# Large attention scores of batches 2 to 7 over 64 rows, two heads side by side in the array

## The chip, the cores and the metric

The kernel runs on one core of a Trainium2 chip. A core has a matrix engine (TensorE, "PE" in the profile, with its weight loads listed apart as "PEld"), VectorE (DVE), ScalarE (ACT), GpSimd (POOL) and SyncE (SP), which issues most transfers. The engines have queues of their own and wait for each other by semaphores. The metric is the device time of one execution in microseconds (us): the median over several executions. A change of under 0.2% is about what can't be told from none.

## The reference

Attention with 8 batches, 8 heads, 576 positions and a head dimension of 64, then a mixer over tokens and channels:

```
scores = q @ k^T / sqrt(64)
mask: 0 <= rel < 32                        for heads 0 to 3  (plain)
      0 <= rel < 128 and rel % 4 == 0      for heads 4 to 7  (dilated)
x = softmax(scores under the mask) @ v     -> (batch, 576, 512)
u = x + (relu(x^T @ w_tok1) @ w_tok2)^T
out = u + relu(u @ w_ch1) @ w_ch2
```

Here rel is the query position less the key position. Input and output are float32; the kernel computes in float16 with sums in float32.

## The kernel before

**Score blocks.** Only blocks near the diagonal are computed, with the keys on the 128 partitions of the output and the queries along the row. For a plain head there are three large blocks of 128 keys x 160 queries, and small blocks for the end. For a dilated head positions are taken by their remainder modulo 4, and the large blocks are four of 128 x 128. The tiles of the large blocks are `sc`, one PSUM bank for each head; the small blocks of both heads of a pair share one bank, `sm`.

**Pairs of heads.** Two heads lie on top of each other: `kt[hp]` holds the transposed keys of pair `hp`, head 0 in rows 0 to 63 and head 1 in rows 64 to 127. `qz[hp]` has the transposed queries twice, at index `h` of its second axis: for head 0 rows 64 to 127 are zero, for head 1 rows 0 to 63. So a score matmul reads all 128 rows of `kt` as weights and all 128 rows of `qz[hp][:, h]`, and the zeros take the other head out of the sum. Pairs 0 and 1 are plain (`scores_plain`), pairs 2 and 3 dilated (`scores_dil`).

**Masks.** In batches 0 and 1 (`veiled`) the mask is added by another matmul into the same bank ahead of the score matmul (L319). In batches 2 to 7 it is multiplied in after the exponential, on POOL.

**The three steps of a pair.** `scores_plain` and `scores_dil` are generators with three steps: head 0's large blocks and its exponential on ScalarE (L340 or L369), head 1's, and then the small blocks with their exponentials (L349 and L352, or L377) and POOL's masks. Other work stands between the steps.

**Banks.** The helper `bank` with the tag "sc" gives the two score banks in turn, and from batch 1 on `sm` takes its turn among them (`small_bank`). Three turns for a pair mean that the bank which holds the small blocks of one pair is head 1's in the next pair, and head 1's bank of one pair is head 0's in the next. A matmul that writes to a bank waits until ScalarE has read what was in it.

**Order of the work.** The order is written out by hand: `interleave` walks through the matmuls of the channel mixer of batch b (`gen_main`: `gp`, L529, and `yp`, L546 and L566) and puts in steps of other batches at given times of a planned clock, where each step has a planned cost. The scores of batch b + 2 stand in the mixer of batch b, from its time 20.6 on, 2.8 apart for the pairs; between them stand the transposes of q and k of the pairs ahead (`transposes`, tiles `tp_q` and `tp_k`, L270, L288 and L290) with their copies into `qz` and `kt` by ScalarE or VectorE. Batches 2 and 3 have times of their own. The instructions of each engine then run in the order in which the program was written.

Of the kernel before, what the change touches and what calls it, by code (L numbers as in the profile page):

```python
# [31 lines left out]
BLK = 160  # L32
# [37 lines left out]
def kernel(  # L70
# [11 lines left out]
    nc = tc.nc  # L82
# [9 lines left out]
    def bank(tag, bufs, name, dtype=FP32):  # L92

        if tag in turn:
            turn[tag] += 1
            tag, bufs = f"{tag}{turn[tag] % bufs}", 1
        return ps.tile([128, 512 if dtype == FP32 else 1024], dtype, tag=tag, bufs=bufs, name=name)
# [13 lines left out]
    def mult(eng, out, a, b):  # L111
        x, y = bass.broadcast_tensor_aps(a, b)
        eng.tensor_tensor(out=out, in0=x, in1=y, op=ALU.mult)  # L113
# [18 lines left out]
    qz = [qza[:, i] for i in range(4)]  # L132
    kta = fixed("kt", [128, 4, 640])
    kt = [kta[:, i] for i in range(4)]
# [181 lines left out]
    def score(b, hp, h, out, keys, queries, hide):  # L316

        if hide is not None:
            nc.tensor.matmul(out=out, lhsT=ident, rhs=hide, start=True, stop=False)  # L319
        nc.tensor.matmul(out=out, lhsT=kt[hp][:, keys], rhs=qz[hp][:, h, queries],  # L320
                         start=hide is None, stop=True)

    def veiled(b, hp):
        return b <= 1

    def small_bank(b, hp):
        return bank("main", 3, f"sm_{b}_{hp}") if b == 0 else bank("sc", 2, f"sm_{b}_{hp}")

    def scores_plain(b, hp):
        a = attp[hp]  # L330
        blocks = a[:, :, 0:PTL].rearrange("p h (b c) -> p h b c", c=PST)
        tl = a[:, :, PTL + 64:PTL + 128]
        veils = veiled(b, hp)
        wide, narrow = (veil[:, 0:BLK], veil[:, 0:64]) if veils else (None, None)
        for h in range(2):
            p = bank("sc", 2, f"sc_{b}_{hp}_{h}")
            for kb in range(3):
                score(b, hp, h, p[:, BLK * kb:BLK * kb + BLK], slice(128 * kb, 128 * kb + 128),
                      slice(128 * kb, 128 * kb + BLK), wide)
            nc.scalar.activation(  # L340
                out=blocks[:, h, 0:3, 0:BLK], in_=p[:, 0:3 * BLK].rearrange("p (b c) -> p b c", c=BLK),
                func=AF.Exp, scale=0.125)
            yield 0.21
        p = small_bank(b, hp)
        for h in range(2):
            score(b, hp, h, p[:, BLK * h:BLK * h + BLK], slice(384, 512), slice(384, 384 + BLK), wide)
        for h in range(2):
            score(b, hp, h, p[:, 320 + 64 * h:384 + 64 * h], slice(512, 640), slice(512, S), narrow)
        nc.scalar.activation(  # L349
            out=blocks[:, :, 3, 0:BLK], in_=p[:, 0:320].rearrange("p (h c) -> p h c", c=BLK),  # L350
            func=AF.Exp, scale=0.125)
        nc.scalar.activation(  # L352
            out=tl, in_=p[:, 320:448].rearrange("p (h c) -> p h c", c=64), func=AF.Exp, scale=0.125)
        if not veils:
            mult(nc.gpsimd, blocks[:, :, :, 0:BLK], blocks[:, :, :, 0:BLK], band)
            mult(nc.gpsimd, tl, tl, band[:, 0, :, 0:64])
        yield 0.21

    def scores_dil(b, hp):
        a = attd[hp - 2]  # L360
        diag = a[:, :, 0:DTL].rearrange("p h (r c) -> p h r c", c=128)
        tl = a[:, :, DTL + 64:DTL + 320].rearrange("p h (x c) -> p h x c", c=128)[:, :, :, 0:64]
        veils = veiled(b, hp)
        for h in range(2):
            p = bank("sc", 2, f"sc_{b}_{hp}_{h}")
            for r in range(4):
                score(b, hp, h, p[:, 128 * r:128 * r + 128], slice(r, 512, 4),
                      slice(128 * r, 128 * r + 128), veil[:, 0:128] if veils else None)
            nc.scalar.activation(out=a[:, h, 0:DTL], in_=p, func=AF.Exp, scale=0.125)  # L369
            yield 0.22  # L370
        p = small_bank(b, hp)
        for h in range(2):
            for x in range(2):
                score(b, hp, h, p[:, 128 * h + 64 * x:128 * h + 64 * x + 64],
                      slice(384 + 128 * x, 512 + 128 * x), slice(512, S),
                      veil[:, BLK + 64 * x:BLK + 64 * x + 64] if veils else None)
        nc.scalar.activation(  # L377
            out=tl, in_=p[:, 0:256].rearrange("p (h x c) -> p h x c", x=2, c=64),
            func=AF.Exp, scale=0.125)
        if not veils:  # L380
            mult(nc.gpsimd, diag, diag, band[:, :, :, 0:128])
            mult(nc.gpsimd, tl, tl, dtail)
        yield 0.12
# [97 lines left out]
    def score_steps(b, t0, dt, offs=(0.0, 0.7, 2.0), places=None):  # L481

        steps = []
        for hp in range(4):
            at, at_s = places[hp] if places else (t0 + hp * dt, t0 + hp * dt + dt)
            for nm in ("q", "k"):
                steps.append((at + 0.9 * (nm == "k"), 0.28, lambda nm=nm, hp=hp: transposes(b, nm, hp)))
            g = (scores_plain if hp < 2 else scores_dil)(b, hp)
            for i in range(3):
                steps.append((at_s + offs[i], 0.21, lambda g=g: next(g)))  # L490
        return steps
# [153 lines left out]
    for jb in range(2):  # L645
        nc.gpsimd.tensor_copy(
            out=w2p[jb], in_=w2[jb][:, 0:512].rearrange("p (m r) -> p r m", r=4))
# [87 lines left out]
    for i in range(3):  # L735
        nc.gpsimd.dma_start(
            out=w4a[:, 4 * i:4 * i + 4],
# [85 lines left out]
```

## Time and profile before

| | before |
|---|---|
| median of 3 runs | 310.94 us (310.69 to 311.1) |
| profiled execution, span | 310.9 us (its only time) |
| TensorE matmul busy | 298.8 us (96%), 3292 |
| TensorE weight loads busy | 268.3 us (86%), 3292 |
| VectorE busy | 168.4 us (54%) |
| ScalarE busy | 152.9 us (49%) |
| POOL busy | 148.4 us (48%) |
| granted clock of TensorE | 1.000 |
| `sc` matmuls, 128 x 160, all batches | 96, 239 ns each |
| `sc` matmuls, 128 x 128, all batches | 128, 220 ns each |

The span is the time from the first to the last instruction of one execution. Matmuls are pipelined, so the durations of neighbours overlap: what a matmul takes of the engine's time is the distance to the start of the next. "Idle before" in a row is the time that the engine had nothing running, with the instruction that ended it. The chain that ended last is followed back from the last instruction; its shares tell whose work sets the time.

### The profile page before, as it was taken

What the parts mean: (1) busy time and instruction counts of PE and PEld (TensorE: products, weight loads), DVE (VectorE), ACT (ScalarE), POOL (GpSimd) and SP (SyncE); (2) the same over time, 40 slices, a digit from 0 to 9 for tenths busy, and PEclk for the clock granted to TensorE, in tenths of its full rate; (3) what the DMA queues carried; (4) which work ended last, traced back from release to release, by engine and by line L of the source; (5) the groups of instructions that cost most, each with busy time, mean ns of one, the idle gap of its engine ahead of it and who ended that gap; (6) DMA issues with size and microseconds to landing.
All of it is one profiled execution on the core that took longest, in us unless ns stands there. A gap on an engine that the chain in (4) does not pass through costs nothing.

```text
span 310.9 us, 8148 instructions
## 1 busy us (share of the span) xinstructions
PE 298.8 (96%) x3292; PEld 268.3 (86%) x3292; DVE 168.4 (54%) x372; ACT 152.9 (49%) x349; POOL 148.4 (48%) x214
## 2 busy tenths in 40 slices
PE   5789999999999999999999999999999999999995
PEld 2677999988988999899987999899987999899884
DVE  5686448756656554655744655555745646523221
ACT  2664436286645635375545635475555635413500
POOL 7872065429970897029930897019940770000000
PEclk9999999999999999999999999999999999999999
DMA  7999999847995529821495129711001130021023
GB/s 216 267 211 180 235 268 291 242 136 215 275 293 126 170 86 289 172 70 60 121 261 136 64 92 306 153 50 57 33 2 27 45 101 3 0 70 67 2 69 103
DMA packets 67606, 43.24 MB, mean 139 GB/s; under 512 B 35920, under 2 KB 66512, under 8 KB 67568
## 3 DMA queue, kind: packets, MB, share of 16 engines
q1 hardware_dynamic: 63328, 37.63, 44.4%
q0 software_dynamic: 2640, 3.91, 7.1%
q10 hardware_dynamic: 1600, 1.18, 1.3%
q8 instruction: 26, 0.43, 0.6%
q14 instruction: 12, 0.10, 0.1%
HBM read 37.04 MB, written 9.44 MB: 149 GB/s over the span
## 4 chain that ended last, share of the span: by engine, by line
PE 91%; DVE 3%; ACT 2%; DMA 2%; issue 1%; ACTq 0%; POOLq 0%
PE gp L529 30%; PE yp L546 26%; PE h1p L426 4%; PE sc L320 4%; PE up L438 4%; PE yp L566 3%; PE tp_q L270 2%; PE tp_k L270 2%; DMA const<-consts 2%; PE sm L320 1%; PE tpu L475 1%; PE av L396 1%; PE h1p L424 1%; PE av L407 1%; PE sc L319 1%; PE tpu L467 1%
## 5 line engine op out<-in xcount | busy, mean ns | idle before, releaser
L529 PE MATMUL gp<-uT,w 128*128 128x288 f16 x768 | 109.9, 286 | 0.7 <-ACT uT L101 0.6
L546 PE MATMUL yp<-w,gt 128*128 128x256 f16 x756 | 93.8, 273 | 0.0
L107 ACT ACTIVATE gt<-gp 128x288 f16<-128x288 f32 x138 | 56.6, 410 | 72.1 <-PE gp L529 65.3
L529 PEld LDWEIGHTS <-w 128*128 128x128 f16 x768 | 83.1, 114 | 8.1 <-issue 1.2
L546 PEld LDWEIGHTS <-gt 128*128 128x128 f16 x768 | 76.0, 106 | 3.9
L113 POOL TENSOR_TENSOR attp<-attp,const 128x1280 f16<-128x1280 f16 (+1 forms) x24 | 35.8, 1515 | 77.8 <-ACT attp L349 67.0
L109 DVE TENSOR_SCALAR gt<-gp 128x288 f16<-128x288 f32 x54 | 24.6, 455 | 35.5 <-PE gp L529 33.9
L556 DVE TENSOR_TENSOR o<-yp,u 128x512 f32<-128x512 f32 x31 | 21.4, 690 | 34.4 <-PE yp L546 34.1
L113 POOL TENSOR_TENSOR attd<-attd,const 128x1024 f16<-128x1024 f16 (+1 forms) x24 | 32.8, 1394 | 0.0
L113 DVE TENSOR_TENSOR xn<-av,rec 128x320 f16<-128x320 f32 x64 | 31.5, 492 | 2.2
L320 PEld LDWEIGHTS <-kt 128*128 128x128 f16 x352 | 27.7, 104 | 3.6 <-DVE kt L275 1.4
L275 DVE COPY kt<-tp_k 128x512 f16<-128x512 f16 x32 | 21.8, 684 | 9.3 <-PE tp_k L270 9.3
L320 PE MATMUL sc<-qz,kt 128*128 128x128 f16 (+1 forms) x224 | 25.8, 228 | 1.0 <-ACT qz L101 0.7
L101 ACT COPY qz<-tp_q 64x576 f16<-64x576 f16 (+1 forms) x32 | 19.9, 621 | 6.1 <-PE tp_q L290 3.6
L340 ACT ACTIVATE attp<-sc 128x480 f16<-128x480 f32 x32 | 17.8, 573 | 9.5 <-PE sc L320 9.0
L445 DVE TENSOR_TENSOR u<-up,xn 128x512 f16<-128x512 f32 x26 | 17.9, 691 | 8.0 <-PE up L438 8.0
L103 POOL CAST c_q<-l_q 128x512 f16<-128x512 f32 x31 | 18.8, 609 | 5.7 <-DMA l_q<-in_q_dram 5.7
L369 ACT ACTIVATE attd<-sc 128x512 f16<-128x512 f32 x32 | 17.9, 596 | 5.8 <-PE sc L320 3.2
L103 POOL CAST c_k<-l_k 128x512 f16<-128x512 f32 x29 | 17.9, 619 | 4.7 <-DMA l_k<-in_k_dram 3.7
L415 DVE RECIPROCAL rec<-av 128x5 f32<-128x5 f32 x64 | 12.2, 191 | 13.2 <-PE av L402 6.9
L103 DVE COPY qz<-tp_q 64x576 f16<-64x576 f16 (+1 forms) x32 | 15.1, 471 | 7.0 <-PE tp_q L288 6.8
L101 ACT COPY uT<-tpu 128x576 f16<-128x576 f16 x15 | 9.6, 640 | 16.3 <-PE tpu L476 16.3
(123 smaller groups left out, 445.1 us busy)
## 6 DMA issues: line engine op xcount, KB each, us to landing
out_dram<-o SPq DMA_DIRECT2D x72, 128.0 KB, 2.0
l_q<-in_q_dram SPq DMA_DIRECT2D x15, 512.0 KB, 5.5
l_k<-in_k_dram SPq DMA_DIRECT2D x14, 512.0 KB, 6.5
l_vn<-in_v_dram SPq DMA_DIRECT2D x32, 128.0 KB, 6.6
l_vd<-in_v_dram SPq DMA_DIRECT2D x16, 256.0 KB, 4.3
w<-in_moe_w_ch_dram POOLq DMA_DIRECT2D x6, 512.0 KB, 7.4
lt<-in_q_dram SPq DMA_DIRECT2D x8, 128.0 KB, 3.9
l_vt<-in_v_dram SPq DMA_DIRECT2D x8, 128.0 KB, 4.8
```

The costliest lines, as they stand in the source:

```text
L101: nc.scalar.copy(out=out, in_=in_)
L103: eng.tensor_copy(out=out, in_=in_)
L107: nc.scalar.activation(out=out, in_=in_, func=AF.Relu)
L109: eng.tensor_scalar_max(out=out, in0=in_, scalar1=0.0)
L113: eng.tensor_tensor(out=out, in0=x, in1=y, op=ALU.mult)
L275: nc.vector.tensor_copy(out=natural(kt[hp][:, 0:512]), in_=main)
L320: nc.tensor.matmul(out=out, lhsT=kt[hp][:, keys], rhs=qz[hp][:, h, queries], start=hide is None, stop=True)
L369: nc.scalar.activation(out=a[:, h, 0:DTL], in_=p, func=AF.Exp, scale=0.125)
L445: nc.vector.tensor_tensor(out=t, in0=p, in1=xn[b][:, s], op=ALU.add)
L529: nc.tensor.matmul(out=p[:, 0:288], lhsT=w3[cb][:, 512 * (mb // 4) + mb % 4:512 * (mb // 4) + 512:4], rhs=uT[(b, cb)][:, 288 * sh:288 * sh ...
L546: nc.tensor.matmul(out=p[:, c], lhsT=gt[(b // 2, mb)][:, a0:m0 + 512:4] if half else gt[(b // 2, mb)][:, a0:a0 + 128], rhs=w4[mb][:, c], s ...
L556: nc.vector.tensor_tensor(out=o32, in0=p, in1=u16[(b, s)], op=ALU.add)
```

## The change

The large blocks of the two heads of a pair are now written together in batches 2 to 7. Both score banks are asked for at once, and the new helper `twin` issues for each block first head 0's matmul, over rows 0 to 63 of `kt` and `qz`, and then head 1's, over rows 64 to 127. The matmuls have 64 rows in place of 128: one uses the upper half of the array's rows and one the lower. The exponentials stay where they stood, head 0's in the first step and head 1's in the second. The small blocks, batches 0 and 1, the zeros in `qz` and the planned times and costs are as before. In `scores_dil` the same is done with four blocks of 128 queries.

```diff
+    def twin(hp, outs, keys, queries):
+
+        for h in range(2):
+            rows = slice(64 * h, 64 * h + 64)
+            nc.tensor.matmul(out=outs[h], lhsT=kt[hp][rows, keys], rhs=qz[hp][rows, h, queries],
+                             start=True, stop=True)
+
...
+        two = None
+        if not veils:
+            two = [bank("sc", 2, f"sc_{b}_{hp}_{h}") for h in range(2)]
+            for kb in range(3):
+                twin(hp, [p[:, BLK * kb:BLK * kb + BLK] for p in two],
+                     slice(128 * kb, 128 * kb + 128), slice(128 * kb, 128 * kb + BLK))
         for h in range(2):
-            p = bank("sc", 2, f"sc_{b}_{hp}_{h}")
-            for kb in range(3):
+            p = two[h] if two else bank("sc", 2, f"sc_{b}_{hp}_{h}")
+            for kb in range(0 if two else 3):
                 score(b, hp, h, p[:, BLK * kb:BLK * kb + BLK], slice(128 * kb, 128 * kb + 128),
                       slice(128 * kb, 128 * kb + BLK), wide)
```

The program has as many matmuls and weight loads as before. Two places show the new order. In these rows `sc_1_0` is the large-block tile of pair 1, head 0, and the number behind it counts tiles; L320 is the score matmul of before, L327 that of `twin`; what stands in brackets is the engine for which the instruction waits.

TensorE, batch 4, pair 1 (plain), before:

```order
L320 LDWEIGHTS kt [waits DVE_49]
L320 MATMUL sc_1_0_3229<-qz,kt 128x160 [waits Activation_49]
L320 LDWEIGHTS kt
L320 MATMUL sc_1_0_3229<-qz,kt 128x160
...
L270 LDWEIGHTS c_q_2813 [waits Pool_49]
L270 MATMUL tp_q_2_3234<-const,c_q_2813 128x128
...
L288 MATMUL tp_q_2_3234<-const,c_t_2799 128x128
L320 LDWEIGHTS kt [waits PE_49]
L320 MATMUL sc_1_1_3243<-qz,kt 128x160 [waits Activation_49]
...
L270 LDWEIGHTS c_k_2828 [waits Pool_49]
```

TensorE at the same place after the change:

```order
L327 LDWEIGHTS kt [waits PE_49,DVE_49]
L327 MATMUL sc_1_0_3229<-qz,kt 128x160 [waits Activation_49]
L327 LDWEIGHTS kt [waits PE_49]
L327 MATMUL sc_1_1_3230<-qz,kt 128x160 [waits Activation_49]
L327 LDWEIGHTS kt
L327 MATMUL sc_1_0_3229<-qz,kt 128x160
...
L270 LDWEIGHTS c_q_2813 [waits Pool_49]
L270 MATMUL tp_q_2_3238<-const,c_q_2813 128x128
...
L270 LDWEIGHTS c_k_2828 [waits Pool_49]
```

Head 1's first matmul, with its wait for ScalarE, has moved from behind the query transposes of pair 2 to the second place of the block, ahead of them.

TensorE, batch 4, pair 2 (dilated), before and then after, where the two heads already stood side by side:

```order
L320 MATMUL sc_2_0_3284<-qz,kt 128x128 [waits Activation_49]
...
L320 LDWEIGHTS kt [waits PE_49]
L320 MATMUL sc_2_1_3290<-qz,kt 128x128 [waits Activation_49]
...
L270 LDWEIGHTS c_k_2828 [waits Pool_49]
```

```order
L327 MATMUL sc_2_0_3284<-qz,kt 128x128 [waits Activation_49]
L327 LDWEIGHTS kt [waits PE_49]
L327 MATMUL sc_2_1_3285<-qz,kt 128x128 [waits Activation_49]
...
L270 LDWEIGHTS c_k_2828 [waits Pool_49]
```

Here head 1's first matmul moves from the fifth place to the second, and nothing else changes its place.

More of the change, by code (lines that the diff above doesn't have):

```diff
@@ L363, in scores_dil @@
         veils = veiled(b, hp)
+        two = None
+        if not veils:
+            two = [bank("sc", 2, f"sc_{b}_{hp}_{h}") for h in range(2)]
+            for r in range(4):
+                twin(hp, [p[:, 128 * r:128 * r + 128] for p in two], slice(r, 512, 4),
+                     slice(128 * r, 128 * r + 128))
         for h in range(2):
-            p = bank("sc", 2, f"sc_{b}_{hp}_{h}")
-            for r in range(4):
+            p = two[h] if two else bank("sc", 2, f"sc_{b}_{hp}_{h}")
+            for r in range(0 if two else 4):
                 score(b, hp, h, p[:, 128 * r:128 * r + 128], slice(r, 512, 4),
```

## The prediction

> **What bounds the kernel now.** I read the page first (span, busy shares, the chain that ended last), then TensorE's list of waits from batch 2's scores to batch 7's, then the groups by shape, then the timelines of TensorE and ScalarE around the changed blocks.
>
> From the page:
>
> ```profile
> span 310.9 us, 8148 instructions
> ...
> PE 298.8 (96%) x3292; PEld 268.3 (86%) x3292; DVE 168.4 (54%) x372; ACT 152.9 (49%) x349; POOL 148.4 (48%) x214
> ...
> PE 91%; DVE 3%; ACT 2%; DMA 2%; issue 1%; ACTq 0%; POOLq 0%
> ```
>
> TensorE is busy 96% of the span and 91% of the chain that ended last is its work. What TensorE waited for between 60 and 250 us, the stretch that holds all changed blocks (total us, times, longest):
>
> ```profile
> PE tpu L475 <- DVE u L445: 0.4, 1, 0.4
> PE gp L529 <- ACT uT L101: 0.4, 1, 0.4
> PE up L438 <- ACT kt L101: 0.3, 1, 0.3
> ```
>
> No wait is on a score bank. So each us added to TensorE's stream from batch 3 on moves the end, and each us removed helps only if no new wait eats it. The groups of the score blocks (batches 0 to 7) and their weight loads:
>
> ```profile
> L320 PE MATMUL sc<-qz,kt 128*128 128x160 f16 x96 | 13.5, 239 | 0.8 <-ACT qz L101 0.7
> L320 PE MATMUL sc<-qz,kt 128*128 128x128 f16 x128 | 12.3, 220 | 0.3 <-DVE kt L275 0.3
> L320 PEld LDWEIGHTS <-kt 128*128 128x128 f16 x352 | 27.7, 104 | 3.6 <-DVE kt L275 1.4
> ```
>
> Now the place itself: batch 4, whose scores run from 134.9 to 145.5 us. TensorE's timeline (start us, us, then the instruction; a new row starts where the kind changes):
>
> ```profile
> 134.90 0.38 PE L320 MATMUL sc<-qz,kt 128*128 128x160 f16 x3
> 135.12 0.39 PE L270 MATMUL tp_q<-const,c_q 128*128 128x128 f16 x4
> ...
> 137.99 0.37 PE L320 MATMUL sc<-qz,kt 128*128 128x160 f16 x3
> 138.19 0.39 PE L270 MATMUL tp_q<-const,c_q 128*128 128x128 f16 x4
> ...
> 138.47 0.37 PE L320 MATMUL sc<-qz,kt 128*128 128x160 f16 x3
> 138.68 0.39 PE L270 MATMUL tp_k<-const,c_k 128*128 128x128 f16 x4
> ...
> 140.69 0.61 PE L320 MATMUL sc<-qz,kt 128*128 128x128 f16 x8
> 141.14 0.39 PE L270 MATMUL tp_k<-const,c_k 128*128 128x128 f16 x4
> ...
> 143.45 0.61 PE L320 MATMUL sc<-qz,kt 128*128 128x128 f16 x8
> ```
>
> Rows overlap, so the price of a block is the distance to the next start: three 160-wide matmuls 0.21 us (138.47 to 138.68), 0.07 each; eight 128-wide ones 0.45 (140.69 to 141.14), 0.056 each. One matmul lasts 219 ns (0.61 less seven steps of 0.056) but the next starts 56 ns after it: a tail of 163 ns is hidden by what follows.
>
> ScalarE at the same place:
>
> ```profile
> 135.38 0.57 ACT L340 ACTIVATE attp<-sc 128x480 f16<-128x480 f32 x1 [0.98 <-PE sc L320]
> 135.84 1.28 ACT L101 COPY qz<-tp_q 64x576 f16<-64x576 f16 x2
> 137.15 0.21 ACT L101 COPY kt<-tp_q 128x64 f16<-128x64 f16 x1
> 137.25 0.58 ACT L340 ACTIVATE attp<-sc 128x480 f16<-128x480 f32 x1
> 137.72 0.45 ACT L349 ACTIVATE attp<-sm 128x320 f16<-128x320 f32 x1
> 138.03 0.30 ACT L352 ACTIVATE attp<-sm 128x128 f16<-128x128 f32 x1
> ...
> 143.05 0.38 ACT L377 ACTIVATE attd<-sm 128x256 f16<-128x256 f32 x1 [0.79 <-PE sm L320]
> ```
>
> From 135.38 to 138.33 it has no pause. The two score banks go round as head 0, head 1, small blocks, head 0 and so on, three turns for a pair: the bank of the small blocks of one pair is head 1's bank in the next. For pair 1 it comes free at 138.33 (138.03 + 0.30). Today head 1 comes to it at 138.47 and doesn't wait. With the change it is wanted by the second matmul, at about 138.0.
>
> **The change, part by part.** *Removed: streaming time.* If a pair of matmuls in the two halves takes the time of one, a plain pair of heads saves 0.21 us and a dilated one 0.225. Six batches with two of each: 6 x (0.42 + 0.45) = 5.2 us at the most. The count of matmuls and weight loads stays.
>
> *Added: 24 blocks in another shape of the array,* so 48 changes between 128 and 64 rows. The trace shows none (every form reads 128*128). Bounds for one change, s: below, 0, since score blocks and transposes follow each other without a gap (138.47 to 138.68); above, the exposed tail of 163 ns and behind it a weight load of 104 ns, 0.26 us. A gain is excluded, for nothing is taken out. Between them lies a weight load alone that can no longer run under the matmul ahead, 0.104. I take s = 0.10, by that row, since a weight load into halves that the old matmul still uses is what surely changes; and keep 0 and 0.26.
>
> The Trainium skill, TensorEngine Tiling (Array Packing), Tiling Modes, Key Properties, speaks against this change: it says that changing the mode, and not only the tile, drains TensorE. No run shown here has such a change, and that section gives no price. The same section has the tiles working in parallel, which is the saving above. The Trainium skill, TensorE: Matmul & The Clock Gate, Part 3, Measured speedup vs the span model, gives 3.07 times for four row tiles; as an estimate from that page two would give 1.53, so 35% saved in place of 50%, and the sum below would end 1.2 us later.
>
> *Moved: head 1's matmuls* ahead of what stood between the heads (query transposes, sometimes six of L546). Those come later by the block and two changes, and so do the ScalarE or VectorE copies behind them; ScalarE's own order is the same. What is new is TensorE waiting for the second bank, with all of its queue behind it. From ScalarE's end to TensorE's start it takes 0.05 us, by this pair of rows (66.59 to 66.64), on ScalarE and TensorE in batch 2:
>
> ```profile
> 66.38 0.21 ACT L101 COPY kt<-tp_q 128x64 f16<-128x64 f16 x1
> 66.64 0.38 PE L438 MATMUL up<-h,w 128*128 128x256 f16 x2 [0.32 <-ACT kt L101]
> ```
>
> *Batches 4 to 7* have the same schedule: the score tiles of batch 4 and of batch 7 (windows of 12 us; busy us and instructions of TensorE and ScalarE) read alike.
>
> ```profile
> 134.00:146.00 12.00, 2.71 (x28) 4.38 (x8) 1.00 0.20 67
> 239.00:251.00 12.00, 2.71 (x28) 4.37 (x8) 1.00 0.23 68
> ```
>
> Pair 0 saves 0.21 and pays 2s, all of it swallowed by pair 1's wait. Pair 1: bank at 138.33 + 0.05 = 138.38; from there 0.21 for the rest of the block, s to change back, 0.28 for the query transposes (138.19 to 138.47), so the key transposes begin at 138.87 + s in place of 138.68: +0.19 + s. Pair 2: 2s - 0.225. Pair 3: its bank is free at 143.43 + 0.05 and is wanted at 143.45 + s + 0.03, no wait: 2s - 0.225. Together 5s - 0.26; four batches: 20s - 1.04.
>
> *Batch 3* has other distances (before, the blocks of pairs 1 to 3 begin at 102.05, 104.84 and 107.35, by the rows below less what lies between, all before their bank is free). TensorE, then ScalarE:
>
> ```profile
> 102.05 0.37 PE L320 MATMUL sc<-qz,kt 128*128 128x160 f16 x3
> 102.26 0.82 PE L546 MATMUL yp<-w,gt 128*128 128x256 f16 x6
> ...
> 103.12 0.39 PE L270 MATMUL tp_k<-const,c_k 128*128 128x128 f16 x4
> ...
> 105.57 0.39 PE L270 MATMUL tp_k<-const,c_k 128*128 128x128 f16 x4
> ...
> 107.58 0.82 PE L546 MATMUL yp<-w,gt 128*128 128x256 f16 x6
> 108.24 0.39 PE L320 MATMUL sc<-qz,kt 128*128 128x128 f16 x4
> 108.46 1.47 PE L546 MATMUL yp<-w,gt 128*128 128x256 f16 x12
> ```
>
> ```profile
> 102.20 0.30 ACT L352 ACTIVATE attp<-sm 128x128 f16<-128x128 f32 x1
> ...
> 104.79 0.27 ACT L352 ACTIVATE attp<-sm 128x128 f16<-128x128 f32 x1
> ...
> 107.48 0.38 ACT L377 ACTIVATE attd<-sm 128x256 f16<-128x256 f32 x1 [1.05 <-PE sm L320]
> ```
>
> Pair 1: 102.55 + 0.21 + s + 0.65 (six of L546) = 103.41 + s, was 103.12: +0.29 + s. Pair 2: 105.11 + 0.22 + s + 0.28 = 105.61 + s, was 105.57: +0.04 + s. Pair 3: 107.91 + 0.22 + s + 0.66 = 108.79 + s, was 108.46: +0.33 + s. Pair 0 is swallowed again. Sum 3s + 0.66.
>
> *Batch 2:* pair 0's change falls into the 0.3 us wait for kt, pair 1's saving into the 0.4 us wait for u (which itself comes 2s later), pairs 2 and 3 pay 4s - 0.45. Sum 6s - 0.45. ScalarE, VectorE and POOL get no more work.
>
> All: 29s - 1.04 + 0.66 - 0.45 = 29s - 0.83. With s = 0.10 it is +2.07 us. The sum is made against the profiled execution, 310.9 us in its span (no other time of it is given), which agrees with the median of 310.94: **313.0 us**. The ends of s give 310.1 and 317.6.
>
> **The rivals.** *Free changes, faster.* With s = 0 the sum is -0.83: 310.1 us. For it: no gap between unlike neighbours in any row above. Against it: no row has another shape. It decides at s = 0.029, where the sum is zero; beyond 0.2% (0.62 us, about what a measurement of this kernel can tell) it is faster only under 0.007 and slower above 0.05.
>
> *Full drain.* Each change exposes the 163 ns tail: 4.73 - 0.83 = +3.9, 314.8 us. For it speaks that nothing of a new shape may be able to enter before the old is out; against it, that the tail may be in part reading and writing, which need no empty array. This is what the rule of the Trainium skill on draining (TensorEngine Tiling (Array Packing), Key Properties) would do here.
>
> *The halves don't overlap,* so the change doesn't do what it says. The saving in pairs 2 and 3 (12 x 0.225 = 2.7) and in what follows the wait of pair 1 (6 x 0.21 = 1.26) is gone: +4.0, 314.0 us with s = 0, 317.0 with 0.10. Against it: separate rows and separate banks; no row here shows it either way.
>
> *The second bank is there in time.* Then the whole 5.2 comes off and 48 changes go on: 4.8 - 5.2 = -0.4, 310.5 us, no change that can be measured. For it would have to hold that ScalarE ends earlier; the unbroken row of seven instructions up to 138.33 speaks against it.
>
> **How the numbers follow.** Forecast with s from 0.05 to 0.13: 0.38. Full drain: 0.15. No overlap: 0.10. All three are slower: 0.63. Between 0.01 and 0.05, or the bank in time: same, 0.14. Free changes, or waits smaller than worked out: faster, 0.23; more than the narrow bound of s would give, since my waits rest on differences of a few hundredths of a us. The range 309.9 to 316.8 takes in the free change and most of no overlap, and leaves out about 1 in 10 at each end, the flush with a bare weight load above it.
>
> **What would show it.** In batch 4's eight matmuls of pair 2 the last should start some 0.2 us after the first (0.39 before); twice that means no overlap. The gap ahead of a block and behind it, beyond the usual 56 ns, is s. The list of waits should have TensorE's score matmuls on ScalarE's L352 of before, about 0.4 us in each of batches 3 to 7. The forecast falls if these waits are absent, or if the blocks stand without gaps.

## The result, and the profile after

The changed kernel takes 314.02 us (median of 4 runs, 313.88 to 314.94), the kernel before in the same comparison 311.02 us (median of 4 runs, 310.69 to 312.2). The ratio is 1.0098, with a 95% interval of 1.0076 to 1.012: slower by about 3.0 us. The forecast was 313.0, with a range of 309.9 to 316.8.

The page of the changed kernel:

```profile
span 313.1 us, 8147 instructions
...
PE 300.7 (96%) x3292; PEld 263.1 (84%) x3292; DVE 168.3 (54%) x372; ACT 152.9 (49%) x349; POOL 148.9 (48%) x214
...
PE 88%; ACT 5%; DVE 3%; issue 2%; DMA 2%; ACTq 0%; POOLq 0%
```

TensorE's share of the chain that ended last has gone from 91% to 88%, and ScalarE's from 2% to 5%. So part of the time is now a wait on ScalarE. TensorE's waits between 60 and 253 us, in the columns of before:

```profile
PE sc L327 <- ACT attp L365: 0.9, 5, 0.3
PE tpu L494 <- DVE u L464: 0.6, 1, 0.6
PE gp L548 <- ACT uT L101: 0.4, 1, 0.4
PE up L457 <- ACT kt L101: 0.3, 1, 0.3
PE sc L327 <- ACT attp L353: 0.2, 1, 0.2
PE sc L327 <- DVE kt L275: 0.2, 1, 0.2
```

L365 is L352 of before, the last exponential of a plain pair's small blocks. Five waits on it are new, one in each of batches 3 to 7, each at pair 1. The list counts only the time in which no matmul was still running; the distance between starts below shows more of it. In batch 3 the second matmuls of pairs 2 and 3 are late too, 0.17 and 0.36 us behind the first and 0.05 behind the exponentials that free their banks; the list does not show these. Batch 4 on TensorE:

```profile
134.10 1.47 PE L565 MATMUL yp<-w,gt 128*128 128x256 f16 x12
135.51 0.38 PE L327 MATMUL sc<-qz,kt 64*128 64x160 f16 x6
135.82 0.40 PE L270 MATMUL tp_q<-const,c_q 128*128 128x128 f16 x4
...
138.59 0.24 PE L327 MATMUL sc<-qz,kt 64*128 64x160 f16 x1
138.99 0.36 PE L327 MATMUL sc<-qz,kt 64*128 64x160 f16 x5 [0.16 <-ACT attp L365]
139.29 0.40 PE L270 MATMUL tp_q<-const,c_q 128*128 128x128 f16 x4
...
141.54 0.22 PE L288 MATMUL tp_q<-const,c_t 128*128 128x128 f16 x1
141.69 0.42 PE L327 MATMUL sc<-qz,kt 64*128 64x128 f16 x8
142.04 0.40 PE L270 MATMUL tp_k<-const,c_k 128*128 128x128 f16 x4
```

Pair 2's eight matmuls last 0.42 us together where they lasted 0.61, so the last starts about 0.2 us after the first: the halves do overlap. But ahead of the block there are 0.15 us from the last transpose (141.54 to 141.69) where a 128-wide matmul is followed after 0.056, and behind it the same (the last couple starts at 141.89, the key transposes at 142.04). From the last transpose to the key transposes it is 0.50 us, and before it was 0.50 too (0.056 and 0.45). Overlap and changes of shape are even. Pair 1's second matmul starts 0.40 us after the first. ScalarE there:

```profile
135.99 0.57 ACT L353 ACTIVATE attp<-sc 128x480 f16<-128x480 f32 x1 [1.05 <-PE sc L327]
...
138.65 0.30 ACT L365 ACTIVATE attp<-sm 128x128 f16<-128x128 f32 x1
```

The second bank came free at 138.95, and 0.04 us later the matmul started.

To see where the time arose, the start of the same instruction is compared in both traces. The profiled execution of before began its first transposes 0.6 us later than that of after (7.01 and 6.41), and the query transposes ahead of batch 2's scores, still ahead of anything that was changed, 0.74 later (64.59 and 63.85). So the spans alone mislead, and the steps count:

| after minus before, us | ahead of the batch's scores | behind them | cost |
|---|---|---|---|
| batch 2 | -0.74 | -0.58 | 0.16 |
| batch 3 | -0.58 | +0.53 | 1.11 |
| batch 4 | +0.53 | +0.93 | 0.40 |
| batch 5 | +0.93 | +1.33 | 0.40 |
| batch 6 | +1.33 | +1.73 | 0.40 |
| batch 7 | +1.73 | +2.14 | 0.41 |

Sum 2.88 us, which agrees with the 3.0 of the medians. Between the batches and behind the last one nothing moves. Within batch 4 nearly all of the 0.40 arises at pair 1: the key transposes behind it go from 138.68 to 139.58, 0.90 later, where everything ahead of the batch's scores was 0.53 later. Pairs 2 and 3 add 0.03 together. Where a cost "by the trace" stands below, it is worked out in this way.

### The profile page after: what moved, and what is told of

Its sections match the earlier page's. It is cut to its first block, busy times and chain, and to the rows that moved or that the text cites. A ratio compares the mean times of both kernels' runs of the same rounds, so it can differ in the third digit from the quotient of the medians.

```text
span 313.1 us, 8147 instructions
## 1 busy us (share of the span) xinstructions
PE 300.7 (96%) x3292; PEld 263.1 (84%) x3292; DVE 168.3 (54%) x372; ACT 152.9 (49%) x349; POOL 148.9 (48%) x214
## 4 chain that ended last, share of the span: by engine, by line
PE 88%; ACT 5%; DVE 3%; issue 2%; DMA 2%; ACTq 0%; POOLq 0%
PE gp L548 30%; PE yp L565 24%; PE h1p L445 4%; PE up L457 4%; PE yp L585 3%; PE sc L327 3%; PE tp_q L270 2%; ACT qz L101 2%; PE tp_k L270 2%; DMA const<-consts 2%; PE tpu L494 1%; PE av L415 1%; PE sm L320 1%; PE h1p L443 1%; ACT attp L362 1%
## 5 line engine op out<-in xcount | busy, mean ns | idle before, releaser
L565 PE MATMUL yp<-w,gt 128*128 128x256 f16 x756 | 93.8, 273 | 0.0
L565 PEld LDWEIGHTS <-gt 128*128 128x128 f16 x768 | 75.9, 106 | 4.4
L320 PEld LDWEIGHTS <-kt 128*128 128x128 f16 x184 | 15.5, 102 | 2.4 <-DVE kt L275 1.4
L107 ACT ACTIVATE h<-h1p 128x256 f16<-128x256 f32 x28 | 10.8, 385 | 10.4 <-PE h1p L445 8.3
```

What stands on the lines that cost most here:

```text
L107: nc.scalar.activation(out=out, in_=in_, func=AF.Relu)
L565: nc.tensor.matmul(out=p[:, c], lhsT=gt[(b // 2, mb)][:, a0:m0 + 512:4] if half else gt[(b // 2, mb)][:, a0:a0 + 128], rhs=w4[mb][:, c], s ...
```

## The experiments

Theory 1 is that of the prediction: the changes of shape eat the overlap, and the waits on the second bank make the loss. Its rivals: the changes alone make the loss, or the waits alone, or a fixed price of a block.

**The order without the shape.** The changed kernel's order, with all 128 rows and the zeros:

```diff
-            rows = slice(64 * h, 64 * h + 64)
-            nc.tensor.matmul(out=outs[h], lhsT=kt[hp][rows, keys], rhs=qz[hp][rows, h, queries],
+            nc.tensor.matmul(out=outs[h], lhsT=kt[hp][:, keys], rhs=qz[hp][:, h, queries],
```

> The changed kernel's order (both banks asked for at once, the heads alternating), but each large matmul over all 128 rows with the zeros of qz, so no change of shape and no overlap: the new waits on the second bank alone. Theory 1 (the loss is made of 48 changes of shape at 0.1 us, new waits on the second bank, less the overlap): in batches 4 to 7 pair 1's second matmul starts at 138.38 on before's clock and five more of 0.07 follow, +0.33 a batch; in batch 3 pairs 1 to 3 wait, +0.43, +0.21 and +0.50; in sum +2.5 us on the kernel before, 313.5. Rival (the changes of shape alone make the loss, the banks come in time): no change, 311.0.

Measured: 314.39 us, ratio 1.0091 (1.0061 to 1.0121); by the trace 3.40 us: 0.29 in batch 2, 1.27 in batch 3 and 0.46 in each of batches 4 to 7. The waits alone cost as much as the whole change; the rival that gives them nothing has fallen. Batch 4 in this kernel, TensorE:

```profile
134.73 0.59 PE L326 MATMUL sc<-qz,kt 128*128 128x160 f16 x6
...
137.85 0.23 PE L326 MATMUL sc<-qz,kt 128*128 128x160 f16 x1
138.35 0.51 PE L326 MATMUL sc<-qz,kt 128*128 128x160 f16 x5 [0.27 <-ACT attp L364]
```

The second matmul of pair 1 starts 0.50 us after the first. The expectation had 0.33 a batch. The 0.13 that was missing: in this order head 0's last matmul in pair 0 is the fifth of six and not the third, so ScalarE's chain starts two matmuls of 0.07 later, and the bank comes free that much later.

**The shape without the order.** The order of before, each head's large blocks over its own 64 rows:

```diff
+    def one_half(hp, h, out, keys, queries):
+        rows = slice(64 * h, 64 * h + 64)
+        nc.tensor.matmul(out=out, lhsT=kt[hp][rows, keys], rhs=qz[hp][rows, h, queries],
+                         start=True, stop=True)
...
-                score(b, hp, h, p[:, 128 * r:128 * r + 128], slice(r, 512, 4),
-                      slice(128 * r, 128 * r + 128), veil[:, 0:128] if veils else None)
+                args = (p[:, 128 * r:128 * r + 128], slice(r, 512, 4), slice(128 * r, 128 * r + 128))
+                score(b, hp, h, *args, veil[:, 0:128]) if veils else one_half(hp, h, *args)
```

> The order of before, but the large blocks of batches 2 to 7 each over their own 64 rows: no two heads alternate, so nothing overlaps but at a head's border, and no bank is asked for earlier. 40 blocks in another shape (6 in each of batches 4 to 7, 8 in batches 2 and 3), 80 changes. Theory 1: 80 x 0.1 = 8.0, less some 0.7 that falls into batch 2's waits, +7.3 us, 318.3. Rival (a change of shape costs nothing that counts, the loss is bank waits): 311.0 to 311.5. Rival (a full drain of 0.163 us for each change): +12, 323.

Measured: 317.04 us, ratio 1.0176 (1.0137 to 1.0215); by the trace 5.89 us. A change of shape has a price. TensorE in batch 4, the end of pair 0 and pair 1:

```profile
139.85 0.82 PE L553 MATMUL yp<-w,gt 128*128 128x256 f16 x6
140.60 0.38 PE L326 MATMUL sc<-qz,kt 64*128 64x160 f16 x3
140.91 0.40 PE L270 MATMUL tp_q<-const,c_q 128*128 128x128 f16 x4
...
143.73 0.43 PE L326 MATMUL sc<-qz,kt 64*128 64x128 f16 x8
```

Six of L546 (here L553) take 0.66 us and are followed after 0.75: 0.09 to 0.10 for the change. Three 160-wide take 0.21 and the next begins after 0.31: 0.10 for the change back. The full drain of 0.163 has fallen. The time is below the 7.3 expected because pairs 2 and 3 of batches 4 to 7 overlapped although their heads don't alternate (the last row: 0.43 us for eight, 0.61 in the kernel before); that is 8 x 0.2 = 1.6 us. The run with the heads one after the other, below, looks at it.

**The small blocks in other banks,** to have the second bank free in time, with a control:

```diff
-        return bank("main", 3, f"sm_{b}_{hp}") if b == 0 else bank("sc", 2, f"sm_{b}_{hp}")
+        return bank("main", 3, f"sm_{b}_{hp}") if b != 1 else bank("sc", 2, f"sm_{b}_{hp}")
```

> The changed kernel, but the small blocks of batches 2 to 7 go to the three banks of the channel mixer, so that the second score bank is free when the pair of blocks wants it. Theory 1: the waits on ScalarE's last exponential are gone; what is left is 48 changes at 0.1 = 4.8 us and about 0.03 us for the slower first pair of each block, 0.7, less the 5.2 of overlap: +0.3 us on its own control (e4_ctrl), within 0.4 either way; about 311.3. Rival (the waits cost little and the changes nearly all of it): still +2.5 to +3.0, 314.

> The kernel before with the small blocks of batches 2 to 7 in the three banks of the channel mixer: the control of e3_bank. Theory 1 and its rivals alike: the banks of the mixer turn one place further for each pair, and TensorE waits for none of them: no change beyond 0.2%, 311.0. If the mixer's banks become tight, up to +1 us, which then stands in e3_bank as well.

Measured: 318.80 us, ratio 1.0231 (1.0186 to 1.0276), and for the control 318.87 us, 1.022 (1.0179 to 1.026). The control was expected even and lost 7.5 us: the mixer's banks are tight. The first rows of TensorE's waits with the changed blocks:

```profile
PE sm L320 <- DVE o L575: 1.7, 4, 0.4
PE gp L548 <- DVE o L575: 1.6, 3, 0.7
PE yp L565 <- DVE o L575: 1.2, 2, 0.7
```

There is no row of `sc` on ScalarE any more, and both kernels take the same time, 0.6 us apart by the trace. This agrees with theory 1, but weakly, since waits of some 4.5 us on these banks stand in both.

**More time between the pairs,** with a control:

```diff
-            steps += score_steps(3, 24.2, 2.8) + at(9.0, 0.6, cast_steps(3))
+            steps += score_steps(3, 21.4, 3.5) + at(9.0, 0.6, cast_steps(3))
...
-                steps += at(2.0, 0.6, cast_steps(b + 2)) + score_steps(b + 2, 20.6, 2.8)
+                steps += at(2.0, 0.6, cast_steps(b + 2)) + score_steps(b + 2, 17.8, 3.5)
```

> The changed kernel with the scores of batches 3 to 7 planned 3.5 apart in place of 2.8, with the same end, so that 0.7 more of the mixer's work lies between the small blocks of one pair and the next pair's blocks. Theory 1 (new waits on the second bank, and changes of shape that eat the overlap): the waits of batches 3 to 7, 0.4 us at each pair 1 and some more in batch 3, are filled with work, and what stays is blocks that cost what they cost before: +0.3 us on e6_space_ctrl, within 0.4. Rival (the wait is not the spacing's, or the changes of shape cost more than the overlap brings): +2 to +3 on e6_space_ctrl.

> The kernel before with the same spacing as e5_space: its control. By both theories TensorE has the same matmuls and no bank is late: 311.0, within 0.5; more only if copies of the transposes now come too close together, which then stands in e5_space as well.

Measured: 315.34 us, ratio 1.014 (1.0095 to 1.0185), and for the control 314.09 us, 1.0096 (1.0067 to 1.0126). By the trace they are 1.85 us apart, where 0.3 was expected, and the control itself was expected even. The edit didn't do what it was for: the planned clock is not TensorE's, and pair 1's block still came 3.09 us after pair 0's in batch 4 (135.27 less 132.18), as before. TensorE's waits with the changed blocks say so, beside a wait on the mixer's sums that both kernels have:

```profile
PE tpu L494 <- DVE u L464: 2.3, 6, 0.6
PE sc L327 <- ACT attp L365: 0.5, 3, 0.2
```

It decides nothing.

**The heads one after the other in a block:**

```diff
-            for r in range(4):
-                twin(hp, [p[:, 128 * r:128 * r + 128] for p in two], slice(r, 512, 4),
-                     slice(128 * r, 128 * r + 128))
+            for h in range(2):
+                for r in range(4):
+                    one_half(hp, h, two[h][:, 128 * r:128 * r + 128], slice(r, 512, 4),
+                             slice(128 * r, 128 * r + 128))
```

> The changed kernel, but within each block head 0's three or four matmuls come first and head 1's behind them, so that the halves do not alternate in the program. If the overlap needs the alternation: the 5.2 us of overlap go, but for the border of the heads (24 x 0.06), of which the waits hide a part: +3 us on the changed kernel, 317. If TensorE takes head 1's matmuls past head 0's, as the eight side by side in e2_halves look: no change on the changed kernel, 314.0 within 0.4, and in batch 4 the last of pair 2's eight starts 0.2 us after the first.

Measured: 314.06 us, ratio 1.0093 (1.0062 to 1.0124), and 2.95 us by the trace, as the changed kernel. Pair 2 of batch 4 on TensorE:

```profile
140.41 0.42 PE L326 MATMUL sc<-qz,kt 64*128 64x128 f16 x8
140.76 0.40 PE L270 MATMUL tp_k<-const,c_k 128*128 128x128 f16 x4
```

In the program head 0's four stand ahead of head 1's four. If they started in that order, head 1's first could not start before head 0's fourth, three steps of 0.056 later, and the eight would last some 0.17 us longer than they do. The starts in the trace come in couples, 14 ns between the two (140.405 and 140.419, 140.488 and 140.502). So head 1's matmuls pass those of head 0 that wait for their half, and the alternation in `twin` isn't needed for the overlap.

Pair 1 still waits for its second bank here, though no wait on L365 stands in TensorE's list. Its block in batch 4:

```profile
137.32 0.75 PE L326 MATMUL sc<-qz,kt 64*128 64x160 f16 x6
```

Six took 0.38 in pair 0 of the changed kernel. The bank came free at 137.67, and the fourth matmul started at 137.71, 0.24 us behind the third. Head 0's matmuls were still in flight for nearly all of that time, which is why the list counts no idle time; the price of the pair is the same (0.36 us, and 0.37 in the changed kernel).

**ScalarE's chain made shorter:** pair 1's copies on VectorE.

```diff
-        eng = nc.scalar if hp == 0 or (hp == 1 and b != 1) or (b == 0 and hp == 3) else nc.vector
+        eng = nc.scalar if hp == 0 or (hp == 1 and b < 1) or (b == 0 and hp == 3) else nc.vector
```

> The changed kernel, with the copies of pair 1's queries (and of its key tail) in batches 2 to 7 on VectorE in place of ScalarE, so that ScalarE's chain ahead of the second bank is 1.3 us shorter. Theory 1: pair 1's wait of about 0.4 us in batches 3 to 7 is gone or nearly so: 1.3 to 2 us less than the changed kernel, 312.0 to 312.7. Rival (the bank is late for another reason, such as TensorE's own small blocks): 314. If VectorE's copies now come late for pair 1's scores, a wait on them shows in TensorE's list.

Measured: 313.39 us, ratio 1.0072 (1.0046 to 1.0097); by the trace 2.18 us, with 0.17 in each of batches 4 to 7 in place of 0.40. Pair 1 of batch 5 on TensorE, then the small exponentials on ScalarE, then the key copy on VectorE:

```profile
171.13 0.82 PE L565 MATMUL yp<-w,gt 128*128 128x256 f16 x6
172.02 0.39 PE L327 MATMUL sc<-qz,kt 64*128 64x160 f16 x6
172.34 0.40 PE L270 MATMUL tp_q<-const,c_q 128*128 128x128 f16 x4
```

```profile
171.39 0.44 ACT L362 ACTIVATE attp<-sm 128x320 f16<-128x320 f32 x1 [1.09 <-PE sm L320]
171.72 0.27 ACT L365 ACTIVATE attp<-sm 128x128 f16<-128x128 f32 x1
```

```profile
171.28 0.68 DVE L275 COPY kt<-tp_k 128x512 f16<-128x512 f16 x1
```

The six matmuls of the block now run without a break, and the gap of 0.40 us is gone. What stays is 0.24 us ahead of the block where a change of shape costs 0.10: the keys are copied at 171.96, because VectorE has the copies ahead of them, and the bank is free at 171.99. So ScalarE's chain set the wait, as theory 1 says; the saving is 0.23 us a batch, 1.15 us in batches 3 to 7, and less than expected, since the copy on VectorE is late next, and since one wait on L365 stays in batch 3. What frees the bank in batch 5 has changed too: ScalarE now idles 1.09 us until TensorE's small blocks are there, which are what the rival named, so copying less on ScalarE would not free it any earlier. Another 0.37 us is lost between the scores of batches 3 and 4, where TensorE now waits for VectorE once more (118.54, for xn).

**Only blocks that don't wait.** Pairs 2 and 3 of batches 4 to 7 as changed, all else as before; and the same with each block cut in three:

```diff
+        two = None
+        if b >= 4:
+            two = [bank("sc", 2, f"sc_{b}_{hp}_{h}") for h in range(2)]
+            for r in range(4):
+                twin(hp, [p[:, 128 * r:128 * r + 128] for p in two], slice(r, 512, 4),
+                     slice(128 * r, 128 * r + 128))
```

> The change at pairs 2 and 3 of batches 4 to 7 alone, 8 blocks whose second bank is free in time; everything else as before. Theory 1 in its present form (a block on its own is even: two changes of 0.096 us and 0.03 for its first pair, against 0.22 of overlap; the loss is waiting for the second bank): within 0.1 us of the kernel before in the trace from batch 4's scores to batch 7's, 311.1 +- 0.4 in time. Rival (a block costs time of its own beside the waits, or brings some): the measured change shared over 24 blocks would give 8 x 0.12, +1.0 us, 312.1.

```diff
+                if r in (0, 3):
+                    twin(...)
+                    continue
+                for h in range(2):
+                    score(b, hp, h, two[h][:, 128 * r:128 * r + 128], slice(r, 512, 4),
+                          slice(128 * r, 128 * r + 128), None)
```

> As e9_dilated, but in each of the 8 blocks only the first and the last remainder run in the two halves, and the two between run over 128 rows: four changes of shape a block in place of two, and half the overlap. Theory 1: two changes more at 0.096 and 0.112 of overlap less, +0.30 us a block, and 0.03 for one more first pair: +2.4 to +2.7 us on e9_dilated. Rival (a change is paid once for a block, as a fixed price of entering it): +0.9 us, the lost overlap alone. Rival (a full drain of 0.163): +3.5.

Measured: the first 311.62 us, ratio 1.0006 (0.9984 to 1.0027), and 0.14 us by the trace over its 8 blocks (0.1 was expected as the most), 0.02 each: a block that doesn't wait is even, to what a time can tell. The cut one 314.54 us, ratio 1.0112 (1.0085 to 1.0139); by the trace 3.00 us, so 0.36 a block more than the first. Pair 2 of batch 4 when cut, on TensorE:

```profile
138.73 0.22 PE L288 MATMUL tp_q<-const,c_t 128*128 128x128 f16 x1
138.88 0.25 PE L327 MATMUL sc<-qz,kt 64*128 64x128 f16 x2
139.06 0.41 PE L320 MATMUL sc<-qz,kt 128*128 128x128 f16 x4
139.41 0.25 PE L327 MATMUL sc<-qz,kt 64*128 64x128 f16 x2
139.59 0.40 PE L270 MATMUL tp_k<-const,c_k 128*128 128x128 f16 x4
```

The price is paid at each change, not once for a block: every one of the four adds about 0.1 us. The 2.9 us between the two kernels by the trace lie a little above the 2.4 to 2.7 that were expected, and below the 3.5 of a full drain. None of the variants is faster than the kernel before.

## Why the prediction was right, step by step

- **The halves overlap: right.** 0.42 us for eight in place of 0.61, and 0.38 for six 160-wide matmuls, where three took as long. The rival of no overlap has fallen. So has the estimate that the prediction drew from the Trainium skill (TensorE: Matmul & The Clock Gate, Part 3, Measured speedup vs the span model), 35% saved in place of 50%: the distance from couple to couple is the 0.056 us of a single matmul, but for the first.
- **A change of shape at 0.10 us: right in size,** 0.15 - 0.056 = 0.096 on either side of a block. The trace agrees with the rule of the Trainium skill (TensorEngine Tiling (Array Packing), Tiling Modes, Key Properties) so far that a change of mode costs; but it is not the whole tail of 163 ns. The old matmul's row ends at 141.76 by the profile, which models the ends of matmuls, 0.07 after the new one starts. That the 0.096 is a bare weight load, the reason given for the choice, isn't shown.
- **A block alone is even: 0.02 by the trace** where 2s - 0.225 gave -0.025. The terms left out are the first couple, which is followed after 0.08 and not 0.056, and the first matmul over 128 rows behind a block, which is followed after 0.067 and not 0.056 by a transpose, and after 0.14 and not 0.11 in L565.
- **The second bank is late at pair 1: right,** five waits in the list, on the exponential that was named, and pairs 2 and 3 of batch 3 as forecast. With ScalarE's chain shortened the break inside the block is gone in batches 4 to 7, and 0.14 us ahead of it are left.
- **The sum was too small, 2.07 for 2.88 by the trace.** Batch 2 was put at 6s - 0.45 = 0.15 and measured 0.16; batch 3 at 3s + 0.66 = 0.96 and measured 1.11. The mis-sized term is that of batches 4 to 7, 5s - 0.26 = 0.24 a batch, which measured 0.40. Its bank was taken as free at 138.33, as before. But ScalarE's chain begins with the exponential of pair 0's head 0, and this waits for a matmul behind a change of shape. The bank came free at 138.95 on a clock that ran 0.53 late: 0.09 later than was put down. Where I said that pair 0's changes are swallowed by the wait, the first of them lengthens it. That is 0.09 in each of batches 4 to 7, and nearly all of what pair 1 cost above its forecast there (0.37 for 0.29). Pairs 2 and 3 bring the rest: 0.01 and 0.02 where -0.025 was put down for each, by the terms left out above. In batch 3 the bank of pair 1 came 0.11 later than was put down, by the same cause.
- **The other rivals.** Free changes fell with the price of 0.096. A bank that is there in time holds for 8 blocks as they stand and gives +0.14 for them; as an estimate from these, over 24 blocks it would be some +0.4 where -0.4 was put down, and no change that can be measured either way.
- **The base.** The prediction took the 310.9 us of the span for the profiled execution's own time. The runs of the changed kernel give both, 313.96 us with a span of 312.2, so about 1.8 us lie outside. The profiled execution of before had a late start, and its span may have come out near the median by that; its own time isn't given. The step itself is a difference and isn't touched.

## What to carry to other kernels

A matmul over half of the array's rows can share its time with one over the other half, but entering and leaving that shape cost about 0.1 us each here, so a block has to save clearly more than 0.2 us, which eight 128-wide matmuls (0.22) do not: make the blocks long, or do without. Work that is drawn together asks for its buffers together, and the buffer that comes last decides; look for who frees it, and whether the change itself delays that engine's first step. And compare traces by the starts of the same instruction ahead of and behind the changed place, since here the two executions were 0.7 us apart before the change came into play.

## What the hardware did that I had not expected

TensorE doesn't keep the program's order between the two halves: with four matmuls of the upper half ahead of four of the lower one in the program, their starts came in couples, 14 ns between the two of a couple, and the time was the same as with alternating ones (314.06 and 314.02 us). With the alternating order the two of a couple start 3 to 5 ns apart. The price of a change of shape was the same after 128-wide transposes and after 256-wide matmuls (0.096 and 0.09 to 0.10 us). What it is made of stays open.
